# Another order of the instructions in the eight-step blocks with one unit of 14 products (two attention layers, gated mix)

## Chip, cores and metric

One core of a Trainium2 chip. The metric is device time in microseconds for one execution. The engines: PE (TensorE, matmuls, with its weight loads shown as PEld), ACT (ScalarE), DVE (VectorE), POOL (GpSimd) and SP (SyncE, which issues DMAs). The program writes one instruction stream for each engine; engines wait for one another by semaphores.

## The reference

Two attention layers with 32 heads of 18 on the same 2048 x 576 input; the first has keys and values of its own for each head, the second shares one key and one value head. A sigmoid gate mixes the two outputs.

```python
def _A_ref(x, wqkv, wo):                       # 32 heads, own k and v
    q, k, v = split(x @ wqkv)
    p = _softmax(einsum("bhqd,bhkd->bhqk", q, k) * Dh ** -0.5)
    return merge(einsum("bhqk,bhkd->bhqd", p, v)) @ wo
...
def _B_ref(x, wq, wk, wv, wo):                 # 32 heads, one shared k and v
    ...
x = A_x
g = _sigmoid((x * gate_w).sum(-1, keepdims=True))
return g * _A_ref(x, A_wqkv, A_wo) + (1 - g) * _B_ref(x, B_wq, B_wk, B_wv, B_wo)
```

## The kernel before

**Steps.** The 64 heads of both layers ("u") are worked off one after the other, each in 16 steps of 128 keys, 1024 steps in all. After a lead-in the kernel emits blocks of eight steps from strings: one letter is one instruction (or one group) on PE, and PE works them off strictly in that order.

- `s` (`step_scores`, L742): one score matmul, 128 keys x 512 queries, on the lower 64 rows of the array. ACT's exp (L750) reads its PSUM bank and writes a tile `pt`, one of 14 in turn.
- `m`, `x`, `y` (`step_max`, L697): a matmul of queries against 512 keys on the upper 64 rows, for the row maxima, which run 22 steps ahead of the scores. `m` and `y` are read by DVE (L706, L703), `x` by ACT (L700, a Relu of the difference of two key blocks, which the `y` that follows adds on DVE). When the 16 query tiles of a head are through, `max_rows` (at the start of every second block) gathers the maxima on DVE, splits them on POOL and sends them by DMA into two rows of the head's query tile `qs`.
- a digit (`step_pv`, L757): so many quarters of the sums of a step, `pt` times values, four matmuls side by side on four column groups, accumulated in the bank `acc`. A step's four quarters read the step's four exps. At the end of a head `head_out` copies `acc` out on DVE.
- `A`, `B` (`half_step`, L965): one product of a unit. A unit is a piece of the projections (292 or 288 columns): 13 of its 14 products on the upper rows (A) and 14 on the lower (B), each half accumulated in a bank of its own. ACT copies A's sum out (L934), DVE adds B's to it (L940).

So between two digits lies a stretch in which the two row halves of the array work side by side, `s` and `B` on the lower half, `m`, `x`, `y` and `A` on the upper one.

**Banks.** Seven PSUM banks serve `s`, `m`, `x`, `y`, `A` and `B`; the eighth is `acc`. Which bank an instruction takes is settled when the program is written: `Clock`, a planner with durations written into the kernel (L41 on), follows the order and gives each instruction the bank that it expects to be free first. While a unit is open, A and B keep one bank each. On the chip the instruction waits by semaphore until that bank has been read.

**Which string where.** `T` is the step at which a block begins. `HALF14` is the string of the blocks that hold one unit of 14 products: `T` from 58 to 210 and from 226 to 722, in eights. Between these stands one `PLAIN` block (no unit), and another follows; the six blocks before have two units (`TWO14`).

```python
elif VB <= T < RB - 8 or RB <= T < RE:
    emit(HALF14, 1)
...
else:
    emit(PLAIN)
```

With `s` at every eighth score matmul `begin(T)` issues what is due at this step: loads of queries and keys on SP's queue, and the slow work on finished heads.

Of the kernel before, what the change touches and what calls it, by code (L numbers as in the profile page):

```python
# [156 lines left out]
def gated_mix_kernel(ctx: ExitStack, tc: tile.TileContext, xT, wall, wv, wo, out):  # L157
# [997 lines left out]
    clk.half = HALF_MM  # L1155

    PLAIN = "mssmsm 4 smsmsm 3 smmssx 3 smmsys 3 mssxysm 3 msxmssm 3 mssysms 3 msssmys 4 msmsms 3 smxssm 3"
    HALF14 = "ysmssm 4 mssmsm 3 smsmsm 3 xsmssm 4 msmssm 3 msAsABABAyBsABAABAsmBABsAABmBABABmBsxmBBxs 3 smmssm 4 mssymss 4 ysxssm 4"
    TWO14 = "xsmsms 5 msssysm 4 smsmms 4 msAsmBABABABBmAsmBABsAABABmBABABmsBAABsm 3 mssmms 4 smxssm 4 ysABBmsAABsABAABmBsABABysAABBAABAsmBmBBxs 4 smxssy 4"
    TWO12 = "xssyms 5 msAsAsAmBBBAABBmsABABmsAABmBABBAAsmBys 3 xssmms 5 smmssm 4 msyssm 3 smsmsm 3 smxsms 5 msAsmsABABABBAysBAABBmsAABAsAmBBABmBsx 4"  # L1160
    HALF12 = "smmsms 4 msmsms 3 xsmssm 3 msmssy 4 mssAABABysABABABmBsAABmBAsABmBBAAsxB 2 msmssm 4 msmssm 2 smms 2 symsxs 4 msysxs 4"
# [75 lines left out]
    while pos["s"] < 4 * (NSTEP - LEAD):  # L1237
# [7 lines left out]
        elif VB <= T < RB - 8 or RB <= T < RE:  # L1245
            emit(HALF14, 1)
        elif RE + 8 <= T < RE + 8 * 9:
# [47 lines left out]
```

## Time and profile before

| | |
|---|---|
| median of 3 runs | 2635.12 us (2633.13 to 2638.15) |
| span of the profiled execution | 2632.7 us |
| PE busy, weight loads | 2619.6 us (99%), 1402.5 us (53%) |
| ACT busy | 2446.7 us (93%) |
| DVE busy | 2395.2 us (91%) |
| POOL busy | 860.7 us (33%) |
| share of PE in the chain that ended last | 96% |

The time of the profiled execution is known as its span alone: from the first to the last instruction that the profile shows, 2.4 us less than the median of the runs. A matmul's end is modelled, and matmuls of the two row halves overlap in the records, so the starts of PE's rows are read here rather than their durations. "PEld" rows are weight loads: the load of a matmul into a bank starts only when the bank is free. In a row of the timeline, the columns are start in us, length in us, engine, line, operation, tiles and count; in square brackets is the idle time before it and what ended it. In a row of the stretches of time: the stretch, its length, busy us and count of PE and of PEld, the granted clock of TensorE, the share of DMA and GB/s.

### The profile page before, as it was taken

How to read it: one execution, taken by the hardware profiler on the slowest of the kernel's cores; microseconds unless marked ns; L12 is line 12 of the kernel's file. 1: busy time of each engine (PE TensorE's matmuls, PEld its weight loads, DVE VectorE, ACT ScalarE, POOL GpSimd, SP SyncE). 2: the span in 40 equal slices, each digit the busy share in tenths (PEclk: the TensorE clock that was granted, in tenths of full speed). 3: DMA queues.
4: the chain of work that ended last, by engine and by line, in shares of the span. 5: the costliest groups of instructions: out<-in, count | busy, mean ns of one | idle time of the engine just before them, and what ended most of it. 6: DMA issues, size and time to landing. Idle time of an engine off the chain costs nothing.

```text
span 2632.7 us, 66902 instructions
## 1 busy us (share of the span) xinstructions
PE 2619.6 (99%) x25197; PEld 1402.5 (53%) x25197; DVE 2395.2 (91%) x4575; ACT 2446.7 (93%) x4862; POOL 860.7 (33%) x1108
## 2 busy tenths in 40 slices
PE   9999999999999999999999999999999999999999
PEld 7655545545555455454554555545555544545665
DVE  6899999999999999999999999999998999999883
ACT  5999999999999999999999999999999999999887
POOL 5611000211365535643554446443310020012113
PEclk9999999999999999999999999999999999999999
DMA  8412111212343234323544344434422332233312
GB/s 255 141 58 61 36 48 56 74 52 72 97 117 112 88 98 116 116 90 93 149 133 138 119 130 148 143 116 123 141 95 76 100 97 85 63 88 123 112 56 93
DMA packets 176520, 270.43 MB, mean 103 GB/s; under 512 B 59161, under 2 KB 137705, under 8 KB 164817
## 3 DMA queue, kind: packets, MB, share of 16 engines
q1 hardware_dynamic: 159125, 211.39, 28.1%
q0 software_dynamic: 16032, 53.25, 5.5%
q8 instruction: 198, 3.24, 0.5%
q10 hardware_dynamic: 1040, 1.52, 0.2%
q14 instruction: 125, 1.02, 0.1%
HBM read 190.26 MB, written 66.90 MB: 98 GB/s over the span
## 4 chain that ended last, share of the span: by engine, by line
PE 96%; DMA 1%; POOL 1%; SPq 1%; issue 0%; ACT 0%; DVE 0%; ACTq 0%; POOLq 0%
PE acc L757 39%; PE bank L697 29%; PE bank L742 17%; PE bank L965 10%; SPq L163 1%; PE acc L769 1%; PE bank L945 1%; DMA xsh<-xT 0%; PE bank L278 0%; DMA ksb<-kq 0%; DMA ke<-pdhl 0%; POOL oacc L938 0%; POOL phl L242 0%; POOL pst L1099 0%; POOL qk L163 0%
## 5 line engine op out<-in xcount | busy, mean ns | idle before, releaser
L750 ACT ACTIVATE pt<-bank 128x512 f32<-128x512 f32 x4096 | 2145.0, 616 | 122.8 <-PE bank L742 71.3
L706 DVE TENSOR_REDUCE mx<-bank 128x1 f32<-128x512 f32 x3002 | 1885.7, 683 | 118.6 <-PE bank L742 58.1
L742 PE MATMUL bank<-qs,ksb 56*128 56x512 f32 x2688 | 906.9, 424 | 1.5 <-DMA qs<-m_d 1.5
L697 PE MATMUL bank<-ksb,qs 54*128 54x512 f32 x2270 | 806.4, 426 | 0.0
L757 PE MATMUL acc<-pt,vb 128*19 128x256 f32 (+3 forms) x6144 | 553.1, 455 | 0.0
L697 PEld LDWEIGHTS bank<-ksb,qs 54*128 54x128 f32 x2270 | 382.8, 184 | 319.8 <-ACT pt L750 191.2
L757 PE MATMUL acc<-pt,vg 128*19 128x512 f32 (+3 forms) x5952 | 535.1, 455 | 0.0
L742 PEld LDWEIGHTS bank<-qs,ksb 56*128 56x128 f32 x2688 | 441.0, 184 | 156.2 <-DVE mx L706 63.9
L742 PE MATMUL bank<-qs,ksa 56*128 56x512 f32 x1408 | 466.7, 425 | 0.0
L697 PE MATMUL bank<-ksa,qs 54*128 54x512 f32 x1232 | 438.6, 426 | 0.0
L703 DVE CUSTOM_DVE_ANT_0 junk<-bank,xb 128x512 bf16<-128x512 f32 x500 | 342.5, 685 | 29.6 <-PE bank L742 24.3
L700 ACT ACTIVATE xb<-bank 128x512 f32<-128x512 f32 x500 | 292.3, 606 | 13.8 <-PE bank L742 3.0
L697 PEld LDWEIGHTS bank<-ksa,qs 54*128 54x128 f32 x1232 | 207.8, 184 | 150.5 <-ACT pt L750 86.6
L240 POOL CAST mh<-mt 128x32 fp32r<-128x32 f32 x63 | 13.2, 210 | 827.4 <-DVE mt L715 605.3
L742 PEld LDWEIGHTS bank<-qs,ksa 56*128 56x128 f32 x1408 | 225.5, 184 | 84.2 <-DVE mx L706 31.3
L757 PEld LDWEIGHTS acc<-pt,vb 128*19 128x19 f32 x6144 | 123.1, 97 | 203.0 <-issue 169.5
L757 PEld LDWEIGHTS acc<-pt,vg 128*19 128x19 f32 x5952 | 119.7, 97 | 206.9 <-issue 180.9
L240 POOL CAST rhl<-rst 128x292 fp32r<-128x292 f32 (+2 forms) x81 | 34.0, 420 | 486.4 <-issue 304.7
L965 PE MATMUL bank<-xr,wrh 64*128 64x292 f32 (+1 forms) x1134 | 168.2, 300 | 0.0
L697 PE MATMUL bank<-kdb,qs 54*128 54x512 f32 x372 | 159.8, 429 | 0.0
L965 PEld LDWEIGHTS bank<-xr,wrh 64*128 64x128 f32 x1134 | 139.5, 186 | 2.8
L560 POOL TENSOR_TENSOR xr<-xst,xr 128x876 fp32r<-128x876 f32 (+1 forms) x63 | 130.5, 2071 | 0.0
(173 smaller groups left out, 2403.4 us busy)
## 6 DMA issues: line engine op xcount, KB each, us to landing
qs<-qk SPq DMA_DIRECT2D x366, 144.0 KB
xst<-xT SPq DMA_DIRECT2D x54, 438.0 KB
ksa<-qk SPq DMA_DIRECT2D x132, 144.0 KB
qk<-rhl POOLq DMA_DIRECT2D x54, 292.0 KB, 4.3
ksb<-qk SPq DMA_DIRECT2D x60, 144.0 KB
qk<-phl POOLq DMA_DIRECT2D x16, 512.0 KB, 5.7
onh<-oh POOLq DMA_DIRECT2D x32, 256.0 KB, 4.4
onl<-ol POOLq DMA_DIRECT2D x32, 256.0 KB, 4.8
```

The source lines that it names most:

```text
L163: return (eng or nc.sync).dma_start(o, i)
L240: eng_h.tensor_copy(h, src)
L560: nc.gpsimd.tensor_tensor(x[:, 5:8, 0:n], t0, x[:, 0:3, 0:n].bitcast(F32), op=OP.subtract)
L697: nc.tensor.matmul(pm, qs[u % 3][b:b + 54, i * P:(i + 1) * P], k, start=True, stop=True)
L700: nc.scalar.activation(MX["x", u, i], pm, AF.Relu)
L703: nc.vector.tensor_tensor_reduce(junk, pm, MX.pop(("x", u, i)), 1.0, -3e38, op0=OP.add, op1=OP.max, accum_out=MX[u][:, i, c:c + 1])
L706: nc.vector.tensor_reduce(MX[u][:, i, c:c + 1], pm, axis=AX.X, op=OP.max)
L742: nc.tensor.matmul(ps, kst(u)[b:b + 56, i * P:(i + 1) * P], qs[u % 3][b:b + 56, c * 512:(c + 1) * 512], start=True, stop=True)
L750: nc.scalar.activation(pt, ps, AF.Exp, scale=SCALE)
L757: nc.tensor.matmul(acc[32 * j:32 * j + 19, a:b], v_of(u, i), PT[u, i, j][:, a:b], start=(i == 0), stop=(i == 15), skip_group_check=True)
L769: nc.tensor.matmul(acc[32 * j:32 * j + 19, 256 * half + a:256 * half + b], v_of(NU - 1, i), pt[:, x + a:x + b], start=(i == 0), stop=(i == ...
L965: nc.tensor.matmul(u.fp[op][:, 0:u.n], x[b:b + 64], y[b:b + 64], start=(n == 0), stop=(n == last))
```

## The change

One string is replaced: the same letters and quarters in another order.

```diff
-    HALF14 = "ysmssm 4 mssmsm 3 smsmsm 3 xsmssm 4 msmssm 3 msAsABABAyBsABAABAsmBABsAABmBABABmBsxmBBxs 3 smmssm 4 mssymss 4 ysxssm 4"
+    HALF14 = "ssmsx 4 msysms 4 smsmms 3 msmsms 3 sxsyms 3 smsmsm 4 mssAmBABAsAABBmsABmBBAsAmBBAsAABBmBBAAsxBys 3 smsyms 4 mssmsx 4 m"
```

Both hold 32 `s`, 24 `m`, 4 `x`, 4 `y`, 13 `A`, 14 `B` and 32 quarters of sums in nine groups. The stretch with the unit is the sixth of nine before and the seventh after; it holds seven `s` before and eight after. Before, one other stretch has four `s` (`mssymss`); after, every other one has three, counting the `m` that ends a block together with the `ssmsx` of the next. The bank of every instruction in these blocks is chosen anew by `Clock`. Nothing else in the kernel is touched.

## The prediction

> **What bounds the kernel now.** I read the page first: engines, then the chain that ended last, then the groups.
>
> ```profile
> span 2632.7 us, 66902 instructions
> ...
> PE 2619.6 (99%) x25197; PEld 1402.5 (53%) x25197; DVE 2395.2 (91%) x4575; ACT 2446.7 (93%) x4862; POOL 860.7 (33%) x1108
> ...
> PE 96%; DMA 1%; POOL 1%; SPq 1%; issue 0%; ACT 0%; DVE 0%; ACTq 0%; POOLq 0%
> ...
> L750 ACT ACTIVATE pt<-bank 128x512 f32<-128x512 f32 x4096 | 2145.0, 616 | 122.8 <-PE bank L742 71.3
> L706 DVE TENSOR_REDUCE mx<-bank 128x1 f32<-128x512 f32 x3002 | 1885.7, 683 | 118.6 <-PE bank L742 58.1
> ...
> L697 PEld LDWEIGHTS bank<-ksb,qs 54*128 54x128 f32 x2270 | 382.8, 184 | 319.8 <-ACT pt L750 191.2
> ```
>
> The chain lies on PE for 96%, but ACT and DVE are busy 93 and 91%: each PSUM bank that PE fills must be emptied by an exp (L750) or a maximum (L706), and the last row shows PE's weight loads held up by exps that have not yet emptied a bank. So the price of an order is PE's own time plus its waits for banks.
>
> How much of the span does the changed order govern? The score matmuls (L742), 32 in each block, counted in the two stretches of time that use it:
>
> ```profile
> 239.35:627.93 388.58, 213.16 (x640) 104.51 (x640) 1.00 0.18 53
> 646.72:1872.93 1226.21, 673.11 (x2016) 329.36 (x2016) 1.00 0.40 118
> ```
>
> That is 20 and 63 blocks, 83 in all, 1614.8 us, 19.455 us each, at the full granted clock (1.00). So 0.064 us per block is 5.3 us, 0.2% of the whole: about what a measurement of this kernel can tell from no change.
>
> Next the timeline of PE over one period, from one unit's stretch to the next. A row is the first matmul of each stretch between two groups of sums (L757):
>
> ```profile
> 1006.24 0.50 PE L697 MATMUL bank<-ksb,qs 54*128 54x512 f32 x1
> ...
> 1010.19 0.84 PE L757 MATMUL acc<-pt,vb 128*19 128x384 f32 x8
> 1010.96 0.50 PE L742 MATMUL bank<-qs,ksb 56*128 56x512 f32 x1
> ...
> 1012.85 0.49 PE L697 MATMUL bank<-ksb,qs 54*128 54x512 f32 x1
> ...
> 1014.97 0.50 PE L697 MATMUL bank<-ksb,qs 54*128 54x512 f32 x1
> ...
> 1016.85 0.49 PE L697 MATMUL bank<-ksb,qs 54*128 54x512 f32 x1
> ...
> 1018.73 0.49 PE L697 MATMUL bank<-ksb,qs 54*128 54x512 f32 x1
> ...
> 1020.39 0.50 PE L742 MATMUL bank<-qs,ksb 56*128 56x512 f32 x1
> ...
> 1022.12 0.49 PE L697 MATMUL bank<-kdb,qs 54*128 54x512 f32 x1
> ...
> 1024.03 0.50 PE L697 MATMUL bank<-ksb,qs 54*128 54x512 f32 x1
> ...
> 1024.37 0.62 PE L742 MATMUL bank<-qs,ksb 56*128 56x512 f32 x2
> 1024.61 0.39 PE L697 MATMUL bank<-ksb,qs 54*128 54x512 f32 x1
> 1024.93 0.85 PE L757 MATMUL acc<-pt,vb 128*19 128x256 f32 x16
> 1025.70 0.50 PE L697 MATMUL bank<-ksb,qs 54*128 54x512 f32 x1
> ```
>
> The period is 19.46 us: the stretch with the unit 4.72, the other eight 14.74. A stretch of three pairs (one matmul on the lower 64 rows, one on the upper, side by side) takes 1.88 with four quarters of sums (1014.97 to 1016.85 to 1018.73) and 1.66 to 1.67 with three (1018.73, 1024.03). The second s of a pair of s starts 0.62 - 0.39 = 0.23 after the first: 0.23 is the slot of one 512-column matmul on its half. From the third pair's start to the sums is 0.32 (1024.61 to 1024.93); three quarters and the change back take 0.77 (1010.19 to 1010.96). What exceeds the plain price is little: 0.06 at 1020.39, 0.03 at 1022.12, and the stretch at 1012.85, with four s, takes 2.12, which is one slot more than 1.88.
>
> The last prices are those of a bank:
>
> ```profile
> 1018.73 0.18 PEld L742 LDWEIGHTS bank<-qs,ksb 56*128 56x128 f32 x1
> 1018.83 0.19 PEld L697 LDWEIGHTS bank<-ksb,qs 54*128 54x128 f32 x1
> ...
> 1019.29 0.60 ACT L750 ACTIVATE pt<-bank 128x512 f32<-128x512 f32 x1 [0.16 <-PE bank L742]
> ...
> 1024.57 1.29 DVE L706 TENSOR_REDUCE mx<-bank 128x1 f32<-128x512 f32 x2 [0.39 <-PE bank L742]
> ...
> 1023.62 2.08 ACT L750 ACTIVATE pt<-bank 128x512 f32<-128x512 f32 x4
> ...
> 1008.61 0.70 PE L965 MATMUL bank<-xr,wrh 64*128 64x292 f32 x6
> 1008.73 0.63 ACT L750 ACTIVATE pt<-bank 128x512 f32<-128x512 f32 x1
> 1009.42 0.18 PEld L697 LDWEIGHTS bank<-ksb,qs 54*128 54x128 f32 x1 [0.17 <-ACT pt L750]
> ```
>
> A lone s loaded at 1018.73 has its exp begin at 1019.29, 0.56 later; an m loaded at 1024.03 has its maximum begin at 1024.57, 0.54 later. An exp holds the bank 0.62 (616 ns), a maximum 0.68. The last two rows are a wait inside a unit's stretch: the exp ends at 1009.36 and the load that wants its bank starts at 1009.42, 0.06 later. So a bank turns once in 1.2 to 1.3 us when its reader is idle. Queued exps follow at (2.08 - 0.62)/3 = 0.49, maxima at 1.29 - 0.68 = 0.61. Products: six begin within about 0.40 us on two halves, some 0.135 each on one half.
>
> **The change part by part.** No instruction is added or removed: both strings hold 32 s, 24 m, 4 x, 4 y, 13 A, 14 B and 32 quarters in nine groups. So nine changes to sums and back, and ACT's and DVE's totals, cost nothing either way: PE's nine changes are there in both. What moves is which matmuls share a stretch, where they stand in it, and, since the planner picks the bank that it expects to be free first, which bank each takes.
>
> Plain stretches. Old: seven of three slots and one of four (mssymss). New: the trailing m joins the next block's ssmsx, so all eight have three slots: five with four quarters, three with three, 5 x 1.88 + 3 x 1.66 = 14.38. One slot is gone: -0.23. Waits: the old eight hold 14.74 - (5 x 1.88 + 3 x 1.66 + 0.23) = 0.13. For the new I set the loads down one after the other with the prices above: the third s of the fourth stretch (msmsms, the third stretch running with three maxima) waits 0.06, the s that ends sxsyms 0.05, another 0.02. So 0.13 again: 14.51.
>
> The unit's stretch. The old one has seven s and 14 B on the lower half, eight m, x, y and 13 A on the upper; the upper is longer, 8 x 0.23 + 13 x 0.135 = 3.6. The new one has eight s and 14 B, 8 x 0.23 + 14 x 0.135 = 3.73: +0.13. To either, 0.11 for the first load, 0.10 to the sums and 0.77 come: 4.58 and 4.71 without waits. Measured is 4.72 in this period; the same operation-by-operation count gives 4.69 for the old order, 19.43 for its whole block against 19.455 measured, so about 0.12 of it is waits.
>
> Now the new stretch's banks. There are seven, and A and B hold two through the unit: five are left. From the first load, in us: m at 0.00 (maximum 0.55 to 1.24, bank out 1.29), s 0.00 (exp 0.60, out 1.27), s 0.11 (exp 1.09, out 1.76), m 0.34 (maximum 1.16, out 1.90), s 0.74 (exp 1.57, out 2.24). All five are taken. The next m stands behind A A B B and could load at 1.15: it waits until 1.27. Everything on PE queues behind it, the products too, which need no new bank. The s behind it takes the m's bank at 1.29. After A B the next m could load at 1.64; the earliest bank is the third exp's, 1.76: 0.12 more. Later s at 2.00, m at 2.24 find banks free, an s at 2.56 waits 0.02, m 2.88, s 3.31, x 3.44, and y waits 0.08 to 3.78. The last s streams at 3.89, sums follow at 4.20, the stretch ends at 4.98: 0.27 of waits, after what the other half makes good. The old order spreads its first tiles wider (m s, A, s, then A B A B A before y) and meets such waits only at its end, as in the row at 1009.42.
>
> Sum per block: -0.23 + 0.00 (plain) + 0.29 (4.98 against 4.69) = +0.06 to +0.08 as I count finely. The count's weak price is when a bank comes free: with exps of 0.65 or a release of 0.08 instead of 0.06 the new order loses 0.16 and 0.17, since it meets a full set of banks more often; nearest the rows is 0.62 with 0.06, so I take +0.09. Times 83: +7.5. Where the order meets a block without a unit (twice), the trailing m stands before mssmsm as a fourth upper matmul: 2 x 0.23 = +0.5. Together +8.
>
> Moved beside it: max_rows now comes right behind the trailing m in DVE's queue, 0.6 us later at most; its rows go by DMA to qs and are wanted six steps later (six eighths of 19.4, 14.6 us), which covers that; without cover the delay would stop PE for the same 0.6 in every second block. The loads that SP issues hang on the step count and move by a stretch at most, with units still 19.4 us apart; POOL is at 33% and prepares the next unit's input one unit ahead. The copy of acc at a head's end still has one three-slot stretch before the next sums. I put all of these at nothing.
>
> The profiled span is 2632.7, 2.4 below the median of the runs, 2635.1; 2635.1 + 8 = 2643.
>
> The ends. Below: if the new stretch has only the old's 0.12 of waits, it takes 4.83, and a block 14.51 + 4.83 = 19.34, -0.09: 2627.6. Above: with the late releases, +0.17: 2649.7; some 3 us more if the sixth stretch (below) waits now and then.
>
> One rule weighed. The rows first: two s in a row, on the same half, start 0.23 apart (1024.37), as do pairs on alternating halves, so a same-half neighbour costs nothing beyond its slot. The Trainium skill, TensorE: Matmul & The Clock Gate, section "Part 3: Packing small matmuls — row/col tiling", says that a weight load overlaps running matmuls only when its row group differs. By that rule every same-half neighbour would pay its load, and the new order has fewer of them; the measured 0.23 does not agree, and my sum goes by the row.
>
> **The rivals.** *Balance wins, faster*: one slot less on PE and no more bank waits than now, because ACT and DVE have the same totals and the shorter plain stretches leave them less backlog at the unit. 2628, as worked out above. Against it: the unit's stretch gets the s that the plain ones lose, and its first five tiles fill all free banks within 0.74 us. It decides if the unit's stretch stays under 4.86 us.
>
> *A wash*: the stretch lands between 4.86 and 4.98, the lost slot and the waits cancel: about 2636.
>
> *Sums wait for an exp*: in the sixth stretch (smsmsm 4) the fourth quarter already needs the exp of that stretch's first s, and the stretch before it has four ACT operations (3 s and x) in 1.66 us, 4 x 0.49 = 1.96. I count that exp ending 1.38 after the stretch's first load; the sums start 0.90 after it (1024.03 to 1024.93) and the fourth quarter 3 x 0.21 later (1.88 less 1.66 is a quarter), at 1.54. Margin 0.16; every 0.1 beyond costs 8.3 us. With 0.1 on top of the forecast: 2651.
>
> *Same-half neighbours cost a load*: counted over a block they fall from 18 to 15. At 0.11 each (second load behind the first, 1018.73 to 1018.83 is the least spacing seen) that is 3 x 0.11 x 83 = 27 us less: 2608. This is the skill's rule as a mechanism; the row at 1024.37 speaks against it.
>
> **How the numbers follow.** Forecast (bank waits in the unit's stretch, 2643): 0.48. Sums wait: 0.09. Balance wins: 0.14. A wash: 0.27. Neighbours: 0.02. Slower by over 0.2%: 0.48 + 0.09 = 0.57; within: 0.27; faster: 0.16. Range 2629 to 2652: the likeliest one's own is 2640 to 2650, the wash lies inside, the balance case nearly all.
>
> **What would show it.** In PE's timeline after, the eight plain stretches should add up to 14.5 a period, none of 2.1; the unit's stretch to 4.95 to 5.05, with loads of L697 waiting on banks behind the second and third group of products. If it is 4.85 or less I was wrong about the banks; if the stretch before the unit is over 1.95, the sums waited for an exp. ACT's and DVE's busy sums should stay, and their waits for PE grow. If PE's row shows nothing of this and the time moves, the cause is one I left at nothing: max_rows, the SP queue or POOL.

## The result and the profile after

The median is 2648.76 us against 2635.12, 13.6 us more. The comparison of all runs gives a ratio of 1.0057 (95% interval 1.0044 to 1.0069), so the change is slower, by about half a percent. The forecast was slower, 2643, with 2652 as the upper end of its range. The profiled execution took 2647.51 us, and its span is 13.0 us longer than before. From the page after, and from its groups of instructions with all releasers:

```profile
span 2645.7 us, 67611 instructions
...
PE 2634.3 (100%) x25197; PEld 1418.8 (54%) x25197; DVE 2404.9 (91%) x4575; ACT 2452.7 (93%) x4862; POOL 860.6 (33%) x1108
...
L742 PEld LDWEIGHTS bank<-qs,ksb 56*128 56x128 f32 x2688 | 440.7, 184 | 196.5 <-ACT pt L750 105.7 <-DVE mx L706 49.3 <-DVE mx L703 12.4
```

ACT and DVE have the same number of instructions and hardly more busy time. Before the score matmuls' loads (L742) PEld stood idle for 196.5 us, most often until an exp ended; before the change, on the page, it was less, and DVE's maxima came first:

```profile
L742 PEld LDWEIGHTS bank<-qs,ksb 56*128 56x128 f32 x2688 | 441.0, 184 | 156.2 <-DVE mx L706 63.9
```

This row does not measure the waits for banks. PEld is idle at the end of each group of sums too, and that pause is put down to the first load of the next stretch, which is an s in four stretches of the new order and in two of the old. Such a load, behind the sums of the unit's stretch:

```profile
1037.55 0.18 PEld L742 LDWEIGHTS bank<-qs,ksb 56*128 56x128 f32 x1 [0.64 <-ACT pt L750]
```

With readers that give the banks back sooner (first experiment) the new order's row still has 193.3 us:

```profile
L742 PEld LDWEIGHTS bank<-qs,ksb 56*128 56x128 f32 x2688 | 441.1, 185 | 193.3 <-ACT pt L750 71.3
```

So the waits have to be read from the places of the loads in time. First, where in the program is the time lost? The 32 score matmuls of each changed block are counted as before the change:

```profile
237.68:629.60 391.92, 220.44 (x640) 104.42 (x640) 1.00 0.18 53
648.96:1884.36 1235.40, 693.70 (x2016) 328.96 (x2016) 1.00 0.40 118
```

1627.32 us for the 83 blocks against 1614.79: 12.53 of the 13.0 us, 19.606 per block against 19.455. The two blocks without a unit that follow them grew by 0.53 (step 218) and 0.72 (step 730); what is left, the rest of the program, is 0.8 shorter. PE's timeline over one block, the first row of each stretch, and the sums that follow the unit's stretch:

```profile
1021.75 0.49 PE L697 MATMUL bank<-ksb,qs 54*128 54x512 f32 x1
...
1023.63 0.49 PE L697 MATMUL bank<-ksb,qs 54*128 54x512 f32 x1
...
1025.52 0.50 PE L742 MATMUL bank<-qs,ksb 56*128 56x512 f32 x1
...
1027.22 0.49 PE L697 MATMUL bank<-ksb,qs 54*128 54x512 f32 x1
...
1028.89 0.50 PE L742 MATMUL bank<-qs,ksb 56*128 56x512 f32 x1
...
1030.62 0.49 PE L742 MATMUL bank<-qs,ksb 56*128 56x512 f32 x1
...
1032.54 0.50 PE L697 MATMUL bank<-ksb,qs 54*128 54x512 f32 x1
...
1036.78 0.84 PE L757 MATMUL acc<-pt,vb 128*19 128x384 f32 x8
1037.55 0.49 PE L742 MATMUL bank<-qs,ksb 56*128 56x512 f32 x1
...
1039.43 0.49 PE L697 MATMUL bank<-ksb,qs 54*128 54x512 f32 x1
...
1041.31 0.49 PE L697 MATMUL bank<-ksb,qs 54*128 54x512 f32 x1
```

No stretch of 2.1 is left; the unit's takes 5.01 (1032.54 to 1037.55). The medians over the 83 blocks are 5.01 against 4.68 for the unit's stretch, and 14.57 against 14.73 for the other eight (the sum of the eight stretches' medians). The waits show in the loads of the unit's stretch, beside the exps whose ends they follow (from ACT's timeline, one window each):

```profile
1032.53 0.18 PEld L697 LDWEIGHTS bank<-ksb,qs 54*128 54x128 f32 x1 [0.21 <-issue]
...
1033.81 0.18 PEld L697 LDWEIGHTS bank<-ksb,qs 54*128 54x128 f32 x1
...
1034.30 0.18 PEld L697 LDWEIGHTS bank<-ksb,qs 54*128 54x128 f32 x1
...
1035.10 0.18 PEld L742 LDWEIGHTS bank<-qs,ksb 56*128 56x128 f32 x1
...
1036.35 0.18 PEld L697 LDWEIGHTS bank<-ksb,qs 54*128 54x128 f32 x1 [0.18 <-ACT pt L750]
```

```profile
1033.16 0.60 ACT L750 ACTIVATE pt<-bank 128x512 f32<-128x512 f32 x1
...
1033.65 0.59 ACT L750 ACTIVATE pt<-bank 128x512 f32<-128x512 f32 x1
...
1035.69 0.60 ACT L750 ACTIVATE pt<-bank 128x512 f32<-128x512 f32 x1
```

The two m behind the product groups load at 1033.81 and 1034.30, 1.28 and 1.77 after the first load, each 0.05 to 0.06 after an exp ends (1033.76, 1034.24). The y loads at 1036.35, 0.06 after the end of an exp at 1036.29.

### The profile page after: what moved, and what is told of

The parts are those of the page before. It is cut to its first block, busy times and chain, and to the rows that moved or that the text cites. A ratio compares the mean times of both kernels' runs of the same rounds, so it can differ in the third digit from the quotient of the medians.

```text
span 2645.7 us, 67611 instructions
## 1 busy us (share of the span) xinstructions
PE 2634.3 (100%) x25197; PEld 1418.8 (54%) x25197; DVE 2404.9 (91%) x4575; ACT 2452.7 (93%) x4862; POOL 860.6 (33%) x1108
## 4 chain that ended last, share of the span: by engine, by line
PE 97%; POOL 1%; DMA 1%; issue 0%; DVE 0%; ACT 0%; ACTq 0%; SPq 0%; POOLq 0%; DVEq 0%
PE acc L757 38%; PE bank L697 26%; PE bank L742 21%; PE bank L965 10%; PE bank L278 1%; PE acc L769 1%; PE bank L945 1%; DMA xsh<-xT 0%; POOL phl L242 0%; POOL pst L1099 0%; POOL oacc L938 0%; DMA wst<-wall 0%; DVE mx L706 0%; POOL qk L163 0%; POOL phl L240 0%
## 5 line engine op out<-in xcount | busy, mean ns | idle before, releaser
L750 ACT ACTIVATE pt<-bank 128x512 f32<-128x512 f32 x4096 | 2172.2, 619 | 136.7 <-PE bank L742 79.1
L706 DVE TENSOR_REDUCE mx<-bank 128x1 f32<-128x512 f32 x3002 | 1912.8, 684 | 147.8 <-PE bank L742 72.8
L742 PE MATMUL bank<-qs,ksb 56*128 56x512 f32 x2688 | 927.1, 429 | 0.3 <-DMA qs<-m_d 0.3
L697 PE MATMUL bank<-ksb,qs 54*128 54x512 f32 x2270 | 820.8, 433 | 0.0
L742 PEld LDWEIGHTS bank<-qs,ksb 56*128 56x128 f32 x2688 | 440.7, 184 | 196.5 <-ACT pt L750 105.7
L697 PEld LDWEIGHTS bank<-ksb,qs 54*128 54x128 f32 x2270 | 378.9, 184 | 302.5 <-ACT pt L750 146.9
L742 PE MATMUL bank<-qs,ksa 56*128 56x512 f32 x1408 | 472.5, 428 | 0.0
L697 PE MATMUL bank<-ksa,qs 54*128 54x512 f32 x1232 | 444.0, 430 | 0.0
L700 ACT ACTIVATE xb<-bank 128x512 f32<-128x512 f32 x500 | 309.6, 619 | 5.9 <-PE bank L742 3.7
L697 PEld LDWEIGHTS bank<-ksa,qs 54*128 54x128 f32 x1232 | 206.9, 184 | 145.5 <-ACT pt L750 71.7
L742 PEld LDWEIGHTS bank<-qs,ksa 56*128 56x128 f32 x1408 | 225.4, 184 | 97.1 <-ACT pt L750 45.9
L697 PE MATMUL bank<-kdb,qs 54*128 54x512 f32 x372 | 156.6, 421 | 0.0
L965 PE MATMUL bank<-xr,wrh 64*128 64x292 f32 (+1 forms) x1134 | 151.7, 298 | 0.0
L965 PEld LDWEIGHTS bank<-xr,wrh 64*128 64x128 f32 x1134 | 124.0, 186 | 0.9
```

The lines of the kernel that those rows point to most:

```text
L697: nc.tensor.matmul(pm, qs[u % 3][b:b + 54, i * P:(i + 1) * P], k, start=True, stop=True)
L700: nc.scalar.activation(MX["x", u, i], pm, AF.Relu)
L706: nc.vector.tensor_reduce(MX[u][:, i, c:c + 1], pm, axis=AX.X, op=OP.max)
L742: nc.tensor.matmul(ps, kst(u)[b:b + 56, i * P:(i + 1) * P], qs[u % 3][b:b + 56, c * 512:(c + 1) * 512], start=True, stop=True)
L750: nc.scalar.activation(pt, ps, AF.Exp, scale=SCALE)
L965: nc.tensor.matmul(u.fp[op][:, 0:u.n], x[b:b + 64], y[b:b + 64], start=(n == 0), stop=(n == last))
```

## Experiments

The theory: PE's own time falls by the slot saved, and more is lost in waits until exps give banks back. Rivals: the doubled products or the eighth s lengthen the stretch by themselves; DVE's maxima hold the banks; the two m in a row do it. The table has the mean of a changed block (first to last block, as above) and the median of the unit's stretch, in us, each from one profiled execution. The edited seam, further below, leaves these blocks' strings as they are in the new order, and has 19.600 against 19.606: that is how closely two such executions agreed. The recorded expectations add up medians, and so reckon a block some 0.03 lower (19.43 before, 19.58 after).

| kernel | block | unit's stretch |
|---|---|---|
| before | 19.455 | 4.68 |
| after | 19.606 | 5.01 |
| old order, light readers | 19.334 | 4.66 |
| new order, light readers | 19.149 | 4.73 |
| new, light exps alone | 19.378 | 4.87 |
| new, light maxima alone | 19.566 | 4.99 |
| new, light x and y alone | 19.509 | 5.01 |
| new, alternating products | 19.565 | 5.01 |
| the same, light readers | 19.148 | 4.73 |
| old, fourth s moved | 19.682 | 5.17 |
| searched order | 19.553 | 4.73 |
| old, six banks | 21.852 | 5.64 |
| new, six banks | 21.859 | 5.98 |

**Light readers.** The same edit on both orders: the exps and the maxima of the `m` read 256 columns in place of 512, so half of that work is left out. The sums stream as many columns as before, and the bank of every instruction stays. Two places of the edit:

```diff
-            nc.scalar.activation(pt, ps, AF.Exp, scale=SCALE)
+            nc.scalar.activation(pt[:, 0:256], ps[:, 0:256], AF.Exp, scale=SCALE)
...
-            nc.vector.tensor_reduce(MX[u][:, i, c:c + 1], pm, axis=AX.X, op=OP.max)
+            nc.vector.tensor_reduce(MX[u][:, i, c:c + 1], pm[:, 0:256], axis=AX.X, op=OP.max)
```

> The old order with light readers: every exp reads and writes 256 of its 512 columns (the sums stream the columns that exist, as many as before), and the maxima of the m matmuls look at 256 of 512 keys. Half of the exps and part of the maxima are left out. PE's instructions and the bank of each stay as they are. Bank theory: a bank comes free about a quarter of a microsecond sooner, the load waits are gone, a unit block takes 19.3 us instead of 19.43. Rival (the shape of the unit's stretch on PE, banks play no part): 19.43 as before.

> The new order with the same light readers, leaving out the same parts. Bank theory: what is left is PE's own time, and there the new order has one slot less: a unit block takes 19.15 to 19.25 us against 19.58 with full readers, the unit's stretch 4.75 to 4.8 against 5.01, and the new order is 0.1 us per block (8 us in all) faster than the old one with light readers. Rival (doubled products and the eighth s make the stretch long by themselves): the unit's stretch stays at 5.0 and the new order stays 0.15 us per block slower.

Score matmuls in the changed blocks, first the old order with light readers, then the new:

```profile
237.62:623.45 385.83, 214.61 (x640) 104.62 (x640) 1.00 0.18 53
641.47:1860.35 1218.88, 675.60 (x2016) 329.56 (x2016) 1.00 0.40 119
```

```profile
240.61:622.77 382.16, 214.65 (x640) 104.75 (x640) 1.00 0.18 54
641.00:1848.17 1207.17, 677.60 (x2016) 329.75 (x2016) 1.00 0.41 120
```

Together these are 1604.71 and 1589.33 us: the sign turns. The whole programs took 2613.0 (0.9918 of before, 0.9901 to 0.9935) and 2597.2 (0.9860, 0.9846 to 0.9875), 15.8 us apart where the blocks are 15.4 apart. A PE timeline row at the start of the new order's unit stretch and of the next one:

```profile
1092.04 0.50 PE L697 MATMUL bank<-ksb,qs 54*128 54x512 f32 x1
...
1096.76 0.50 PE L742 MATMUL bank<-qs,ksb 56*128 56x512 f32 x1
```

That is 4.72. So with light readers the new order is 0.185 us per block better, where 0.1 was expected. What full readers add is 0.457 in the new order (19.606 - 19.149) and 0.121 in the old. The difference, 0.336, less 0.185, is the 0.151 measured. By stretch medians: in the unit's, readers add 0.27 (5.01 - 4.73) in the new and 0.02 in the old; in the other eight 0.16 (14.57 against 14.41) and 0.09 (14.73 against 14.64).

**Which reader.** One half of the edit each, on the new order.

> The new order, only the exps at 256 columns (half of the exps left out), maxima whole. Bank theory: the banks that the two m of the unit's stretch wait for are those of exps, and the wait in the stretch after a long run of exps is an exp's too: a block takes 19.35 to 19.45, the plain stretches after the exp runs fall to 1.67. Rival (DVE's maxima hold the banks): 19.55.

> The new order, only the maxima of m at 256 keys (half of the keys left out of them), exps whole. Bank theory: the waits for exps' banks stay: 19.52 to 19.56, no more than 0.06 less than 19.58. Rival (DVE's maxima hold the banks): 19.40 or less.

Light exps alone take 0.23 off the block and light maxima alone 0.04, but both together 0.46: some 0.19 goes only when both are light. The exps are what the loads wait for first: in the trace after, both `m` of the unit's stretch load right behind the end of an exp in all 83 blocks. When exps alone are light, the maxima are next, and 0.13 of waits is left in the unit's stretch (4.87).

The stretch before the unit's shows this best. It takes 1.92 against 1.88 with light readers, and stays at 1.92 with either half of the edit. Its third `m` loads right behind an exp's end in 77 of the 83 blocks; with light exps it loads right behind a maximum's end in all 83. It is a load that waits there, not a sum that waits for an exp: from the first of its sums to the next stretch it is 0.99 with full and with light readers alike.

**The run of exps.** The third stretch (smsmms) took 1.73, against 1.665 with light readers. Rows of ACT: the first exp of the unbroken run that ends there, and its last, and the load of that stretch's third s:

```profile
1020.48 0.60 ACT L750 ACTIVATE pt<-bank 128x512 f32<-128x512 f32 x1 [0.39 <-PE bank L742]
...
1025.27 0.71 ACT L750 ACTIVATE pt<-bank 128x512 f32<-128x512 f32 x1
```

```profile
1026.03 0.18 PEld L742 LDWEIGHTS bank<-qs,ksb 56*128 56x128 f32 x1
```

The load follows the end of the 0.71 exp (1025.98) by 0.05. The edit gives x (Relu) and the y that uses it 256 columns, so that the run breaks. Its line for x:

```diff
-            nc.scalar.activation(MX["x", u, i], pm, AF.Relu)
+            nc.scalar.activation(MX["x", u, i][:, 0:256], pm[:, 0:256], AF.Relu)
```

> The new order, only ACT's four x operations in a block (and the y on DVE that use them) at 256 columns, which leaves half of the keys out of those maxima; all exps whole. It breaks the run of ten exps that begins before the block's end. Theory (in an unbroken run each exp holds its bank 13 ns longer than the one before, which is what makes the loads of the third stretch wait): the third stretch falls from 1.73 to 1.67, the unit's stretch, whose banks are those of exps early in a run, stays at 5.0; a block 19.50 to 19.54. Rival (the third stretch is long because of its two m in a row): it stays at 1.73.

The third stretch fell to 1.665, the unit's stayed at 5.01. The two m in a row are still there, so they are not the cause. The edit also lets the exps behind an x start earlier, so it does not tell the longer exp from the queue in front of it. Nor is a long run needed for such a wait: the old order's third stretch takes 1.73 as well, against 1.67 with light readers, and its last m loads right behind an exp of 0.61, the third of a run, in all 83 blocks.

**Order of the products.** In the new order: `mssAmBABAsBABAmsBAmBABsAmBABsABABmABABsxBys` for the unit's stretch, with full and with light readers.

> The new order with the doubled products of the unit's stretch (AABB, BBA) made alternating (ABAB), s, m, x and y after as many products as before. Bank theory: the waits for banks shrink to about 0.1 us, but alternating products no longer fill the half that an s or an m leaves idle, and the stretch does not get shorter: 5.0 to 5.1, a block 19.6 to 19.7. Rival (the doubled products are what makes the stretch long): 4.8, a block 19.4.

> The new order with alternating products and light readers (exps at 256 columns, maxima of m at 256 keys; the other halves are left out): what the alternation alone costs PE. Bank theory: without bank waits the doubled products are the better packing, alternating ones take 4.90 to 4.95 in the unit's stretch against 4.73, a block 19.3. So the 5.0 of the alternating order with full readers would be 0.1 of waits on 4.9, that of the new order 0.27 on 4.73. Rival (doubling costs PE time): 4.73 or less.

The unit's stretch at its start and at the next one's, full readers, then light ones:

```profile
1131.23 0.49 PE L697 MATMUL bank<-ksb,qs 54*128 54x512 f32 x1
...
1136.23 0.50 PE L742 MATMUL bank<-qs,ksb 56*128 56x512 f32 x1
```

```profile
1089.07 0.50 PE L742 MATMUL bank<-qs,ksb 56*128 56x512 f32 x1
...
1093.79 0.50 PE L742 MATMUL bank<-qs,ksb 56*128 56x512 f32 x1
```

These are 5.00 and 4.72, the same as the doubled products take. Doubling neither costs, as the rival had it, nor helps, as I had expected; full readers add 0.27 to both. My count for the alternating order, 4.90 to 4.95 with light readers, missed. It let an instruction that is held up on one half hold up the products of the other, which may be too strict; no run tests that alone.

**One part alone.** The old order with the fourth s of `mssymss` moved into the unit's stretch (`BmABAB` to `BmBsABAB`, `mssymss` to `mssyms`).

> The old order with one part of the change alone: the fourth s of mssymss put into the unit's stretch (BmABAB becomes BmBsABAB), so that no stretch but the unit's has more than three slots. If the slot alone counted: a block 19.43 - 0.23 + 0.07 = 19.27. Bank theory: the eighth s meets full banks there and the unit's stretch grows by more than the slot: 5.1, a block 19.6 to 19.7, slower than the new order, which at least arranges the stretch for eight s.

The block took 19.682, as the bank theory had it: the stretch grew by 0.49, not by a slot. The whole program's single run, 2653.28 us, lies within the new order's runs (2647.51 to 2655.24), so here the blocks decide. In the trace the last s of the stretch loads right behind the end of ACT's copy of A's sum in all 83 blocks, and the last m and x before it load behind an exp or a maximum. So moving the s into the unit's stretch costs waits, and the rest of the new order wins part of it back.

**One bank less.** `first()` of the planner chooses among six banks.

> The old order with six banks in place of seven for the planner to give out, nothing left out. Bank theory, the other way round from the light readers: one bank less puts waits into nearly every stretch, a unit block takes 21.7 to 22.0 us, its stretch 5.5 to 5.8. Rival (banks play no part): 19.43.

> The new order with six banks. Bank theory: it needs the seventh more than the old one does, a unit block takes 22.0 to 22.3 us, its stretch 6.0 to 6.3, that is 0.2 to 0.3 us more than the old order with six, where it was 0.15 more with seven. Rival: 19.58.

The unit's stretch, PE's row at its start and at the next one's, old order, then new:

```profile
1164.99 0.49 PE L697 MATMUL bank<-ksb,qs 54*128 54x512 f32 x1
...
1170.63 0.50 PE L742 MATMUL bank<-qs,ksb 56*128 56x512 f32 x1
```

```profile
1167.98 0.50 PE L697 MATMUL bank<-ksb,qs 54*128 54x512 f32 x1
...
1173.97 0.49 PE L742 MATMUL bank<-qs,ksb 56*128 56x512 f32 x1
```

The seventh bank is worth 2.3 to 2.4 us per block. But the two orders come out equal, where I had expected the new one 0.2 to 0.3 behind. Against its time with light readers and seven banks the new order loses 2.71 and the old one 2.52, so the new one loses only 0.19 more, about its advantage. That part of the expectation missed. With six banks the waits have spread: six of the old order's nine stretches and seven of the new one's are longer than with seven. Why they come out even was not tested further.

**The seam.** The block at step 218 begins `ssmsm` and ends `3 m`.

> The new order with one edit at a seam: the block without a unit at step 218 begins with ssmsm and ends with m, so that the m that ends the block before it makes a third pair there and not a fourth upper matmul. It took 18.80 before and 19.33 after. Reckoned with in the forecast was one slot, 0.23; if the seam is all of it, it falls to 18.6 to 18.8; the other such block, at 730, is left as it is and stays at 19.28.

It took 18.76 against 19.33, and the one at 730, left alone, 19.27. The seam at step 218 was worth 0.57 us, not 0.23: its first stretch fell from 2.28 to 1.88 and the next one from 1.94 to 1.75. With light readers the fourth upper matmul costs 0.22 there (2.10 against the old order's 1.88), its slot alone, so the rest is waits.

**An order set down from the prices.**

```diff
+    HALF14 = "smmssm 4 smsyms 3 smmsms 3 smxsms 4 msmsys 3 sAmBBAsAmBABsAAABAsmBBAsAmABBABABmBxsmBBxs 3 smsmsm 4 symsssm 4 smysxs 4"
```

> An order of the same instructions set down with the prices of the traces (a bank is free 0.05 us after its reader ends, exps end 490 ns apart in a run): old frame, with the unit's stretch opening s A m B B A and s and m spread among the products. Bank theory: no wait in the unit's stretch, 4.70, block 19.37 to 19.41, 2 to 5 us faster than the old order in all. Rival: no order of this kind beats the old one, 19.43 or more.

It missed: 2642.59 us, 1.0028 of before (1.0017 to 1.0040), better than the new order and worse than the old. The unit's stretch took 4.73, near the expected 4.70, but `smxsms` took 1.94 and `smysxs` 1.93 (the old order's stretches in these places 1.91 and 1.88). The third s of `smxsms` loads right behind an exp's end in all 83 blocks and that of `smysxs` right behind a maximum's; so does the last s of the unit's stretch behind ACT's copy of A's sum. The prices did not foresee these waits. None of the orders tried here, with full readers, beats the old one.

## Why the prediction was right

The direction and the main mechanism were right: the new order saves PE's own time and loses more than that in waits for banks. The size came out at 13.0 us of span against 8, and several terms were off in ways that partly cancel.

- *One slot less in the plain stretches, -0.23.* With light readers they went from 14.64 to 14.41. Right.
- *PE's own time in the unit's stretch, +0.13.* With light readers it went from 4.66 to 4.73, +0.07.
- *Bank waits in the unit's stretch.* The count gave loads at 1.27, 1.76, 2.56 and 3.78 after the first and an end at 4.98. The rows have 1.28, 1.77, 2.57 and 3.82 and an end at 5.01, and full readers add 0.27, as counted. The old order's 0.12 was wrong: full readers add 0.02 there, the rest is PE's own time. These two slips nearly cancel, which is luck: +0.29 was forecast for the stretch, and +0.32 came.
- *The same waits, 0.13, in the plain stretches of both.* This is the mis-sized term: 0.09 in the old order and 0.16 in the new, so +0.07 per block where the sum has 0.00. The old 0.13 came from prices rounded down: they add up to 14.61 for its eight stretches, which take 14.64 with light readers. For the new order the count had the 0.05 of sxsyms right. The 0.06 that it put into the fourth stretch did not come, but 0.06 in the third and 0.03 in the sixth did. The third stretch waits as long in the old order (0.06), so the longer exps of the new order's long run do not make the difference between the two; the fifth and sixth do, where the load follows the third exp of a run, 0.61 long.
- *From the count to the forecast.* The count gave +0.06 to +0.08 per block, and +0.09 was taken; no row stands behind that step. The forecast's case of late exps (+0.16 per block) lies near the +0.151 that came, but by chance: loads follow an exp's end by 0.05, and in the waits that set the orders apart exps took 0.59 to 0.61, not 0.65. The 0.06 per block that the forecast lacks makes 5 us over 83 blocks.
- *Seams, +0.5.* Measured were 0.53 + 0.72; the m there costs waits beyond its slot.
- *What I put at nothing* (max_rows, SP, POOL, the copy of acc). PE's score matmuls waited 0.3 us in all for the DMA of the maxima's rows, so no late rows show. The blocks that begin with max_rows took 19.624 and the others 19.590, against 19.460 and 19.451 before. So some 1 us of the 13 may go with them (0.025 x 41), about the scatter of one trace; the copy of acc, which also comes in every second block, is not told apart from it. SP and POOL were not tested by a run of their own.
- *The row at the start.* The idle time of the L697 loads, from which the prediction read that exps hold the loads up, is no measure of that (319.8 us before, 318.2 in the old order with light readers). The waits read from the loads' places are.
- *Rivals.* Balance wins is what PE does with light readers, so its one wrong step was that waits would not grow. The sums did not wait for exps: the sixth stretch's sums took 0.99 with full and with light readers. That same-half neighbours cost a load was priced for a fall from 18 to 15 of them in a block. The strings have 18 and 16, so at 0.11 each it would give 0.22 per block on top of the slot's 0.23. With light readers the whole gain is 0.185. In the unit's stretch, where the new order has 11 such neighbours and the old one 8, it would cost 0.33, and 0.07 came. The rule that this rival goes by, of the Trainium skill (TensorE: Matmul & The Clock Gate, "Part 3: Packing small matmuls — row/col tiling"), is that a weight load overlaps running matmuls only when its row group differs. The runs do not bear it out.

## What to carry to other kernels

Where PE and its two readers are all above 90%, an order costs its own time plus its waits for PSUM banks, and the two can change in opposite directions, as here. Halving the readers' work in both versions shows them apart; a row of summed idle time before the loads does not. Set down when each bank is taken and given back in the crowded stretch, before moving a tile there; here a tile taken from a stretch with free banks and put where an accumulation holds two of them cost 0.49, for a slot of 0.23. The order of the products mattered less (0.04) than which stretch a tile is in.

## What the runs showed of the hardware

In an unbroken run of ACT's exps (with the x between them) the starts are 477 ns apart and the ends 490. The first two take 597 and 592 ns, and from there each takes some 13 ns longer. The eleventh (the ninth exp, behind two x), which the new order reaches in each of its changed blocks, has a median of 713 ns, while the old order's runs there go, with two exceptions, no further than the seventh, at 658. So a bank is given back later at the end of a run, though ACT's pitch seems constant by its starts.

A bank's next load follows the end of its reader by 0.05 us (median over the waits behind exps). When one reader is shortened, the wait for the other takes its place: half the exps' work was worth 0.23 us per block, half the maxima's 0.04, and both 0.46.
